# A hash-masked attention kernel with a feed-forward layer: first pair prepared head by head, two more pairs hashed together, and every part of the preparation placed anew

## The chip, the cores and the metric

The kernel runs on one core of a Trainium2 chip. The metric is the device time of one execution in microseconds (us), the median of several. The profile of a kernel is one such execution; its span is about 1.8 us shorter than the device time of the same execution. The engines are TensorE (PE; PEld are its weight loads), VectorE (DVE), ScalarE (ACT), GpSimd (POOL) and SyncE (SP), which here only issues DMAs.

A program on one core shows no second die to compare with, so the state of an execution is judged by its time and by its granted TensorE clock.

## The reference

Attention with a hash as its mask, then a feed-forward layer with the activation h + sin²(αh)/α:

```python
q_bits = (np.einsum('bhsd,dk->bhsk', q, proj) > 0)       # 6 bits; k the same
mask = q_bucket[:, :, :, None] == k_bucket[:, :, None, :]
scores = scale * np.matmul(q, k.transpose(0, 1, 3, 2))
scores = np.where(mask, scores, -1000000000.0)
attn = softmax(scores)                                    # cut
x = np.matmul(attn, v)            # batch 4, heads 8, 768 positions, 64 wide
h = x @ w_in                      # 3072 x 512 by 512 x 2048
g = h + np.sin(alpha * h) ** 2 / (alpha + 1e-09)
return g @ w_out                  # 3072 x 512
```

## The kernel before

The 32 heads are worked in 16 pairs, four pairs to a batch. A pair takes 12 attention steps; a step is one score tile (768 queries by 128 keys), one Exp on ACT and, three steps later, one weighing by the values. After pairs 4, 8, 12 and 15 come 16 steps of the feed-forward layer's first product for the batch before, each with one Sin. Steps are counted through: pairs 0 to 4 are steps 0 to 59, the first feed-forward stretch is 60 to 75, pair 5 is 76 to 87, pair 6 is 88 to 99, pair 9 begins at 140, and so on up to 239; the last 16 Sins follow. The second product is cut into single matmuls, and one or two of them are put into each attention step as filling.

Each pair needs preparation: load, turn (DVE transposes), cast to 16 bits (POOL), hash (PE), find the bits (DVE), and bring queries and keys with their bits into an operand buffer in transposed form. Pairs 0 to 5 are flipped on PE. Pairs 6 to 15 use DMA transposes, a write of the bit rows to memory and a read back. All of these are placed by a table, `PLAN`, from part and pair to a step number; the parts of one step are put into the program after that step's Exp:

```python
for key, when in sorted(PLAN.items(), key=lambda kv: (kv[1], kv[0])):
    at.setdefault(int(when), []).append(key)
...
def go():
    for key in at.pop(now[0], ()):
        part(key)
    now[0] += 1
...
# kinds of part: lq lk lv load; tq tk turn; cq ck cast queries, keys; cv sv cast, sum values;
# hash, bits; rows write bit rows; rq rk read them back; Tq Tk DMA transposes;
# mq mk move the second head; f00..f11 flips on PE; base; wl wc load, cast weights
```

So a step number sets an order in each engine's list. It sets no time. Every buffer is one of a small ring, and a part that takes a buffer waits for the last reader of what lay in it:

```python
hash_pool = ctx.enter_context(tc.tile_pool(name="hash", bufs=2))
aug_pool = ctx.enter_context(tc.tile_pool(name="aug", bufs=3))    # operand buffers qa, ka
v_pool = ctx.enter_context(tc.tile_pool(name="vp", bufs=4))       # values, 16 bits
...
def transpose_by_dma(i, t):
    nc.sync.dma_start_transpose(out=aug_of(i)[t][:, 0, :]..., in_=nats[i, t]...)   # cut
def move_second_head(i, t):
    a = augs[i][t]
    nc.vector.tensor_copy(out=a[0:64, 1, :], in_=a[64:128, 0, :])
```

All DMAs of loads, transposes, rows and results are issued by SP, in one ordered list.

The softmax here doesn't subtract the row's maximum and nothing guards it: scores larger than these inputs give would overflow.

## Time and profile before

| | before |
|---|---|
| median of the first three executions | 315.48 us (313.41 to 316.59) |
| span of the profiled execution | 314.0 us |
| PE / ACT / DVE / POOL busy | 298.0 / 237.9 / 201.4 / 98.2 us |
| first Exp, step 12, first Sin (step 60) | 10.52, 22.49, 63.51 us |
| first feed-forward stretch (steps 60 to 78) | 24.39 us |
| mean granted clock of the profiled execution | one slice of 40 at 0.7, the others full |

PE is busy 95% of the span, so the time can only fall where PE waits or runs at half clock. Read the table by steps: the difference of two step times is the cost of that stretch. This is the view of groups by form of the kernel before, DVE only, from 61 to 93 us: line, engine, operation, output and input, count, then busy us and mean ns, then idle time before.

```profile
L560 DVE SCALAR_TENSOR_TENSOR g<-s,inv_alpha,banks 128x768 bf16<-128x768 bf16 x16 | 16.1, 1014 | 1.1 <-ACT s L588 0.2
L590 DVE TENSOR_TENSOR s<-s 128x768 bf16<-128x768 bf16 x9 | 5.7, 632 | 0.0
```

The stretch's own DVE work is 16 closings (g) and 9 squares, 21.8 us of some 24.4.

### The profile page before, as it was taken

The page shows a single profiled execution, that of the slowest core. Times are in us where ns is not written, and L with a number is a line of the kernel's source. Part 1 is how long each engine was busy: PE and PEld are TensorE (multiplying, and loading weights), DVE is VectorE, ACT ScalarE, POOL GpSimd, SP SyncE. Part 2 cuts the span into 40 slices and gives each one's busy share as a digit, 9 for nine tenths or more (in the row PEclk, how much of TensorE's full clock was granted, in tenths as well). Part 3 has the DMA queues.
Part 4 walks back from the last instruction along what each step waited for, and adds up shares of the span by engine and source line. Part 5 has one row for each costly group of instructions (what it writes and reads, how often), then busy time and mean ns, then how long its engine had stood idle before and what let it go on. Part 6 is the DMA issues. An engine that isn't in the chain of part 4 may idle for free.

```text
span 314.0 us, 7658 instructions
## 1 busy us (share of the span) xinstructions
PE 298.0 (95%) x3026; PEld 184.5 (59%) x3055; DVE 201.4 (64%) x348; ACT 237.9 (76%) x295; POOL 98.2 (31%) x180
## 2 busy tenths in 40 slices
PE   7799989899999998899999999999999999999996
PEld 6467767566555565565656666566556655555444
DVE  4587676689956922769983753869973324499411
ACT  1589989799887788469988878869988887499200
POOL 6757488426695432515000605320000000000000
PEclk9999999999999999799999999999999999999999
DMA  7935989999737596781007697881006202200021
GB/s 232 378 117 157 240 280 294 148 279 252 255 78 214 98 215 163 188 223 26 2 0 201 140 233 126 227 106 21 0 35 106 69 20 76 58 2 0 31 102 70
DMA packets 68724, 42.87 MB, mean 137 GB/s; under 512 B 46560, under 2 KB 63696, under 8 KB 68688
## 3 DMA queue, kind: packets, MB, share of 16 engines
q1 hardware_dynamic: 68576, 42.37, 52.4%
q8 instruction: 24, 0.39, 0.5%
q14 instruction: 12, 0.10, 0.1%
q10 hardware_dynamic: 112, 0.01, 0.0%
HBM read 28.01 MB, written 7.27 MB: 112 GB/s over the span
## 4 chain that ended last, share of the span: by engine, by line
PE 80%; DVE 10%; DMA 3%; issue 2%; POOL 2%; ACT 1%; SPq 0%; DVEq 0%; POOLq 0%; ACTq 0%
PE banks L573 25%; PE banks L608 23%; PE banks L538 16%; PE banks L518 10%; PE banks L293 4%; PE banks L398 2%; DVE qt L284 1%; DMA ka<-kn 1%; DVE g L560 1%; DVE osb L616 1%; DMA proj_sb<-in_proj_dram 1%; DVE kt L284 1%; DMA xt<-xn 1%; DVE qa L400 1%; DVE xn L492 1%
## 5 line engine op out<-in xcount | busy, mean ns | idle before, releaser
L545 ACT ACTIVATE e<-banks 128x768 bf16<-128x768 f32 x192 | 147.7, 813 | 34.7 <-PE banks L538 28.7
L608 PE MATMUL banks<-w_out_bf,g 128*128 128x512 bf16 (+1 forms) x371 | 99.3, 372 | 4.7 <-DVE osb L616 3.3
L538 PE MATMUL banks<-qa,ka 76*128 76x384 bf16 x384 | 93.2, 326 | 0.6 <-DVE ka L400 0.5
L573 PE MATMUL banks<-xt,w_in_bf 128*128 128x384 bf16 x512 | 85.2, 326 | 0.5 <-DVE g L560 0.3
L518 PEld LDWEIGHTS <-e 128*128 128x128 bf16 x1152 | 55.7, 98 | 27.9 <-issue 1.4
L573 PEld LDWEIGHTS <-w_in_bf 128*128 128x128 bf16 x512 | 49.7, 98 | 33.8 <-issue 1.0
L560 DVE SCALAR_TENSOR_TENSOR g<-s,inv_alpha,banks 128x768 bf16<-128x768 bf16 x64 | 64.2, 1013 | 5.2 <-ACT s L588 1.8
L582 ACT ACTIVATE s<-banks,alpha_sb 128x768 bf16<-128x768 f32 x64 | 57.2, 893 | 11.4 <-PE banks L573 9.2
L518 PE MATMUL banks<-vaug,e 128*128 128x65 bf16 x1152 | 62.0, 194 | 0.3
L608 PEld LDWEIGHTS <-g 128*128 128x128 bf16 x400 | 38.6, 97 | 35.8 <-issue 5.3
L486 DVE TENSOR_TENSOR total<-banks,base 128x390 f32<-128x390 f32 x28 | 15.7, 561 | 45.1 <-PE banks L518 44.9
L325 POOL CAST vaug<-v 128x768 bf16<-128x768 f32 x16 | 13.6, 850 | 72.5 <-PE banks L518 32.3
L538 PEld LDWEIGHTS <-ka 76*128 76x128 bf16 x384 | 28.3, 98 | 8.5 <-issue 0.3
L616 DVE COPY osb<-banks 128x512 f32<-128x512 f32 (+1 forms) x25 | 16.7, 668 | 24.5 <-PE banks L608 23.4
L588 ACT ACTIVATE s<-s 128x768 bf16<-128x768 bf16 x29 | 24.5, 843 | 0.9
L590 DVE TENSOR_TENSOR s<-s 128x768 bf16<-128x768 bf16 x35 | 20.9, 597 | 1.9 <-ACT s L582 1.9
L335 POOL TENSOR_TENSOR vacc<-vacc,vaug 128x130 f32<-128x130 f32 x48 | 20.8, 433 | 3.8
L284 DVE STREAM_TRANSPOSE qt<-q 128x768 f32<-128x768 f32 x16 | 15.3, 959 | 2.3 <-DMA q<-in_q_dram 2.3
L492 DVE TENSOR_TENSOR xn<-total,rden 128x384 bf16<-128x384 f32 x28 | 16.1, 575 | 1.0
L293 PE MATMUL banks<-qt,w_hash 128*32 128x192 f32 x128 | 12.9, 331 | 2.5 <-DVE base L342 0.8
L284 DVE STREAM_TRANSPOSE kt<-k 128x768 f32<-128x768 f32 x16 | 15.1, 945 | 0.1
L293 PE MATMUL banks<-kt,w_hash 128*32 128x192 f32 x128 | 12.7, 330 | 0.4 <-DVE kt L284 0.4
(63 smaller groups left out, 177.6 us busy)
## 6 DMA issues: line engine op xcount, KB each, us to landing
q<-in_q_dram SPq DMA_DIRECT2D x16, 384.0 KB
k<-in_k_dram SPq DMA_DIRECT2D x16, 384.0 KB
v<-in_v_dram SPq DMA_DIRECT2D x16, 384.0 KB
out_dram<-osb SPq DMA_DIRECT2D x23, 256.0 KB
w<-in_moe_w_in_dram SPq DMA_DIRECT2D x8, 512.0 KB
w<-in_moe_w_out_dram SPq DMA_DIRECT2D x8, 512.0 KB
rows<-bits SPq DMA_DIRECT2D x40, 24.0 KB
qa<-rows SPq DMA_DIRECT2D x20, 18.0 KB
```

The costliest lines, as they stand in the source:

```text
L284: nc.vector.transpose(out=t.rearrange("p h s b c -> p (h s b c)"), in_=src.rearrange("p h s d -> p (h s d)"),)
L293: nc.tensor.matmul(out=ps[32 * j:32 * j + 32, 0:SB * 32].rearrange("p (s c) -> p s c", s=SB), lhsT=w_hash[:, blk].rearrange("p l a -> p (l ...
L335: nc.gpsimd.tensor_tensor(out=dst, in0=vacc[:, sb % 2], in1=vaug[:, :, sb], op=ALU.add)
L518: nc.tensor.matmul(out=regions[:, qb * (D + 1):(qb + 1) * (D + 1)], lhsT=e[:, qb * 128:(qb + 1) * 128], rhs=vaug[:, hh, kb, :], start=(apa ...
L538: nc.tensor.matmul(out=sc[:, half, 0:HALF], lhsT=ka[0:KA, hh, kb * 128:(kb + 1) * 128], rhs=qa[0:KA, hh, half * HALF:(half + 1) * HALF], s ...
L545: nc.scalar.activation(out=e.rearrange("p (h c) -> p h c", h=2), in_=sc[:, :, 0:HALF], func=AF.Exp, scale=SCALE,)
L560: nc.vector.scalar_tensor_tensor(out=g[:, F, :].rearrange("p (h c) -> p h c", h=2), in0=s2.rearrange("p (h c) -> p h c", h=2), scalar=inv_ ...
L573: nc.tensor.matmul(out=h[:, half, 0:HALF], lhsT=w_in_bf[:, p, F * 128:(F + 1) * 128], rhs=xt[b][:, p, half * HALF:(half + 1) * HALF], star ...
L582: nc.scalar.activation(out=s.rearrange("p (h c) -> p h c", h=2), in_=h[:, :, 0:HALF], func=AF.Sin, scale=alpha_sb[:, F:F + 1],)
L588: nc.scalar.activation(out=s2, in_=s, func=AF.Square)
L590: nc.vector.tensor_tensor(out=s2, in0=s, in1=s, op=ALU.mult)
L608: nc.tensor.matmul(out=o, lhsT=g[:, F, sub * 128:(sub + 1) * 128], rhs=w_out_bf[:, F, c0:c1], start=(F == 0), stop=(F == NF - 1),)
```

## The change

The intent, as it can be read from the diff: let the first pair start sooner by preparing one head before the other, with its queries and keys loaded first; hash pairs 2, 3 and 6, 7 together; and give each part the place that a schedule model found for it. The table keeps its form, but nearly every number in it is new. The diff is cut to its core; the tables of pairs 6, 8, 10 and 12 stand for all.

```diff
 for name, when in dict(          # pair 6
-    lq=30.0241, lk=30.0242, lv=30.0243, cv=51.0066, sv=51.0067, tq=54.0068, tk=54.0069,
-    cq=54.007, ck=54.0071, Tq=54.0072, Tk=54.0073, hash=58.0074, bits=58.0075, rows=58.0076,
-    base=58.0077, mq=77.0078, mk=77.0079, rq=79.008, rk=79.0081,
+    lk=0.04, lv=0.13, lq=0.16, cq=16.01, ck=22.02, cv=31.01, tk=36.01, tq=41.01, sv=42.01,
+    Tq=51.04, Tk=54.01, base=55.02, hash=57.01, bits=60.01, mq=61.01, mk=64.03, rows=69.01,
+    rk=71.02, rq=72.02,
 # pair 8
-    cq=94.0103, ck=94.0104, Tq=94.0105, Tk=94.0106, hash=98.0107, bits=98.0108, ...
+    cq=75.02, Tk=75.05, Tq=77.01, hash=79.01, bits=80.01, cv=80.02, mq=88.01, ...
 # pair 10
-    cv=115.0133, ..., cq=118.0137, ck=118.0138, Tq=118.0139, Tk=118.014, ...
+    ck=80.04, cv=90.01, Tk=99.02, cq=102.01, Tq=108.01, ...
 # pair 12
-    cv=155.0167, ...
+    cv=100.01, ...
-HASHED = {8: (8, 9), 10: (10, 11), 12: (12, 13), 14: (14, 15)}
+HASHED = {8: (8, 9), 10: (10, 11), 12: (12, 13), 14: (14, 15), 2: (2, 3), 6: (6, 7)}
+SQUARES = ('DDADDADAADADADAD', 'AADDADADADAADADD')
+RATES = (1.8397, 1.9304)
+DUMMIES = (23, 6, 6, 0)
...
-        load(0, "q")
-        hash_constants()
-        load_alpha()
-        load(0, "kv")
+        nc.scalar.dma_start(out=proj_sb, in_=proj)
+        load(0, "qk", slice(0, 1))
+        load(0, "qk", slice(1, 2))
+        hash_constants()
...
+        under_way = prepare_first()      # a generator: head 0 now, head 1 in parts later
+        next(under_way)
```

## The prediction

> **What bounds the kernel now.** I read the page's busy table and slices first, to find the busiest engine; then busy times by stretch, to see where it is not full; then TensorE's waits and the timeline at the two places where the stretches show a hole.
>
> ```profile
> PE 298.0 (95%) x3026; PEld 184.5 (59%) x3055; DVE 201.4 (64%) x348; ACT 237.9 (76%) x295; POOL 98.2 (31%) x180
> ...
> PE   7799989899999998899999999999999999999996
> ...
> PEclk9999999999999999799999999999999999999999
> ```
>
> TensorE is busy 95% of 314.0 us, and there is one slice (the seventeenth, 125.6 to 133.4 us) with a granted clock of 0.7. A busy PE need not be a full one, so I add up what its stream must take from the spacing of matmul starts in the trace: scores 384 x 0.162 = 62.2; weighing by values 1152 x 0.029 = 33.4; first feed-forward product 512 x 0.162 = 82.9; second 368 x 0.216 + 32 x 0.109 = 83.0; hashes 8 pairs alone x 0.86 and 4 twos x 1.44 = 12.6; head transposes 144 x 0.056 = 8.1; bit picks 6 x 0.33 = 2.0; base rows 14 x 0.067 + 4 x 0.17 = 1.6. Sum 285.8 us. Real work starts at 5.9 us and the last matmul ends at 310.9, so 305 us are used: about 19 us are lost in the stream, 6 before it and 3 (last copy and store) after it. The change hardly touches the sum, so its gain must come out of these 28.
>
> ```profile
> 0.00:10.50 10.50, 7.52 (x113) 6.50 (x114) 5.15 (x17) 2.28 (x3) 7.69 (x28) 1.00 0.83 271
> 10.50:22.50 12.00, 10.32 (x167) 6.75 (x166) 9.34 (x17) 9.06 (x13) 6.73 (x12) 1.00 0.65 225
> ...
> 51.00:61.60 10.60, 8.81 (x154) 6.16 (x143) 7.95 (x17) 8.44 (x13) 7.25 (x12) 1.00 0.92 186
> 61.60:84.30 22.70, 22.35 (x150) 13.44 (x150) 20.01 (x26) 20.52 (x25) 9.96 (x9) 1.00 1.00 289
> ...
> 112.30:138.00 25.70, 23.08 (x248) 13.96 (x251) 13.30 (x27) 17.74 (x23) 9.47 (x18) 0.93 0.77 183
> 138.00:159.60 21.60, 21.55 (x146) 13.06 (x146) 19.53 (x26) 19.59 (x23) 5.27 (x9) 1.00 0.19 41
> ```
>
> Columns: the stretch, its length, then busy time of PE, weight loads, DVE, ACT and POOL, clock, DMA share, GB/s. The holes in PE are at the start, before 61.6 and in 112 to 138. The two stretches of the feed-forward layer (61.6 to 84.3, 138.0 to 159.6) have nearly none, but there DVE and ACT are both at 88 to 91%.
>
> ```profile
> PE banks L608 <- DVE osb L616: 3.3, 3, 2.3
> ...
> PE banks L340 <- DVE bits L371: 0.9, 1, 0.9
> PE banks L293 <- DVE base L342: 0.8, 1, 0.8
> PE banks L398 <- DVE nat L385: 0.7, 1, 0.7
> PE banks L293 <- DVE qa L400: 0.7, 1, 0.7
> PE banks L293 <- DVE xn L492: 0.6, 1, 0.6
> ```
>
> Columns: who waits for whom, total us, times, longest. All are waits for DVE: PE takes its instructions in order and stands before one part of the preparation (hash, pick, flip) whose DVE predecessor is not through. The longest, 2.3 us:
>
> ```profile
> 121.12 1.29 SPq L412 DMA_TRANSPOSE ka<-kn  x1
> ...
> 125.56 0.35 DVE L427 COPY ka<-ka 64x768 bf16<-64x768 bf16 x1 [2.57 <-DMA ka<-kn]
> 125.83 0.68 DVE L616 COPY osb<-banks 128x512 f32<-128x512 f32 x1
> ...
> 126.56 1.23 PE L608 MATMUL banks<-w_out_bf,g 128*128 128x512 bf16 x3 [2.34 <-DVE osb L616]
> ```
>
> DVE is held by a copy of pair 9's keys that needs a DMA transpose issued only at 121.12; behind it stands the eviction that frees PE's output bank. The chain of waits goes further back: POOL's value cast for pair 9 began at 114.87, then its sums and casts, then the transpose.
>
> **What the Trainium skill says.** "TensorE: Matmul & The Clock Gate", the section "Part 1: The HAM clock gate", has a matmul stream at half clock until some 3.4 us of activity, spaced by N/2.4 + 2.5 ns after. The trace agrees: the warm-up matmuls are 107 ns apart until 3.94 us and 56 ns after; 384 columns 162 ns, 512 columns 216 ns. The page wants an idle window of about 3.4 us for the fall back; here 2.5 us of idle before 126.56 were enough, as 512-column matmuls are 427 ns apart afterwards, until about 130.3. The same page's "Architectural detail" section calls ACT and DVE strict FIFO; the blocked eviction above is that. "ScalarE: Activation LUTs", section "What ACT_TABLE_LOAD costs", gives an ACTIVATE 186 + 0.833 N ns (826 for 768), 93 more with a pointer operand, and back-to-back ones overlap by about 93: the trace has 813 (Exp), 893 (Sin, a pointer scale) and 147.7/192 = 0.769 us per Exp in a row. "DMA: Bandwidth & Descriptors", section "Latency and other measured facts", puts a fixed cost of about 2 us on a DMA: the first 384 KB of queries, issued at 0.74, were usable at 4.04.
>
> **The change part by part.**
>
> *Start.* Before: queries at 4.04, two DVE transposes of 0.97 until 6.07, hash weights by eight POOL copies 4.32 to 6.12, hash done 7.0, bits 7.44, pick and its copy 8.38, flips and copies, first score 9.99, first Exp 10.52. After: one head of q and k is the same 384 KB, so both by about 4.1 (estimate from the old landing); half transposes of 0.49 until 4.7; hash weights by two tiny matmuls and one DVE product (proj is there at 4.2), about 4.95; hash of two rows about 0.65, 5.6; bits 0.42, 6.1; pick 0.33 and a half-sized copy 0.3, 6.9; two flips of 0.34 and a 0.55 copy, 8.3. First score near 8.4, Exp near 8.9: 1.6 us. The warm-up shrinks from 44 dummies to 23 + 6 + 6, which may leave part of this at half clock, up to 0.5 us: I take 1.3.
>
> *Pairs 0 to 4 (60 attention steps).* An Exp cadence of 0.769 makes 46.1 us of ACT; from 10.52 to the end of the sixtieth Exp at 62.2 it took 51.7, so 5.6 are lost: 2.7 in the first 12 steps (22.49 - 10.52 - 9.23), 2.8 in the other 48 (39.7 - 36.9). In the first 12 steps DVE is the limit. I counted its parts after the change: three half or split pieces of pair 0's second head 0.49 + 0.3 + 0.42 + 0.3, its two copies 1.1, pair 1's transposes 1.9, bits and pick copy 0.9, four copies 2.2, and four transposes of pairs 2 and 3, 3.8: 11.4 us against 9.2 of Exp. Thus the head start is mostly eaten there: step 12 some 1.2 us earlier, not 3. The later waits (0.8, 0.9, 0.7, 0.6 us) are what a placement can mend; I give 2.0 of the 2.8. Hashing 2, 3 and 6, 7 together saves 2 x (2 x 0.86 - 1.44) = 0.6 on PE, inside that. Pairs 0 to 4 in sum: 3.2.
>
> *First and second feed-forward stretch.* Square counts are unchanged (7 on ACT and 9 on DVE; 8 and 8 in the last). But DVE gets a key transpose of 0.95, two moves of 0.35 to 0.4 and two copies of 0.55 in the first stretch, and up to five moves, 1.8, in the second, where it already ran without a gap from 140.5 to 162.3. Part falls in its idle while the first Sin is awaited (1.7 and 1.3 us). I charge 0.3 + 0.5 = 0.8.
>
> *The stall of pair 9.* Its query cast goes from plan position 106 to 50, keys to 80, transposes to 86 and 88, the key move to 135. This removes 2.34 us of idle and the half clock of 126.56 to 130.3, that is 3.7/2 = 1.9: 4.2. The parts that come in its place have longer leads, so I give it nearly whole: 4.0.
>
> *The rest.* Waits of 0.5 and 0.6 us at 82 to 89 and 0.5 at 257.8; the faster fill (1.84 instead of 1.75 matmuls a step) only shifts PE work that must be done anyway. I take 1.0. Base rows folded in at the last key block instead of the first: no cost, only a later need.
>
> Sum: 3.2 (the start is in it, by way of step 12) + 4.0 + 1.0 - 0.8 = 7.4. 315.5 - 7.4 = 308.1, rounded 308.0. I add nothing for new waits and nothing for those that I leave standing and a plan searched against a model may have closed: they pull opposite ways.
>
> **Rivals.** (1) New waits eat the gain. For it: many parts lie close to their need (row reads of pair 12 at position 175 for a start at 176, of pair 15 at 227 for 228; weight casts at 75 to 77 just as the second product begins), and the DMA queue is one ordered line in which early loads stand before buffers that come free late. Against it: each engine runs through its own list, so a late position need not be a late time, and PE is up to three score tiles ahead of ACT. Result 311 to 316. (2) DVE becomes the bound in the feed-forward stretches: 20.9 us of its own work for 16 chunks against PE's 20.8, plus the added 2 to 3. Result 310 to 312. (3) The plan fills nearly all holes: ACT's floor met in pairs 0 to 4 (another 2 us), all single waits gone. Result 303 to 305. I hold the middle likelier than any of the three, and (3) likelier than (1), since most of the gain sits in two visible places.
>
> **Range and chances.** 2% is 6.3 us, a time of 309.2. My centre lies 1.2 under it with an uncertainty of about 3.5 (the three runs of before spread over 3.2 us alone). That gives faster 0.64, within 0.34, slower 0.02; eight in ten: 303.5 to 312.
>
> **What would show it.** First Exp near 8.9 us; step 12 near 21.3; first Sin near 60.3 instead of 63.5; no DVE wait of over 1 us for a DMA transpose and no slice of clock 0.7; feed-forward stretches 0.3 to 0.5 longer, DVE above 92% in them. Wrong if PE shows new waits for row reads, weight casts or evictions of over 2 us in sum, or a second fall of the clock.

## The result, and the profile after

The kernel after took 330.35 us (median of 4: 326.68 to 334.58) against 315.21 for the kernel before beside it (median of 4). The ratio is 1.0445, with a 95% interval of 1.0334 to 1.0556: slower. Ratios in this document are the mean time of one kernel's fast runs over that of the other's fast runs of the same rounds, so they are not quite the ratio of the medians that are quoted.

The header, the busy row of PE and the row of the granted clock on the page of the kernel after, in 40 slices of 8.2 us:

```profile
span 327.8 us, 7715 instructions
...
PE 303.6 (93%) x3047; PEld 185.9 (57%) x3074; DVE 205.5 (63%) x361; ACT 238.4 (73%) x297; POOL 96.2 (29%) x173
...
PEclk9999999999999799997999999999999999999999
```

PE's busy time grew by 5.6 us although its work is nearly the same, which fits the falls of the clock: there are now two slices at 0.7 where the kernel before had one. TensorE's waits in the kernel after (who waits for whom, total us, times, longest):

```profile
PE banks L701 <- DVE g L688: 3.6, 3, 1.7
PE banks L646 <- DVE total L615: 3.0, 1, 3.0
PE banks L701 <- DMA xt<-xn: 2.7, 2, 2.4
PE banks L367 <- POOL vsum L362: 2.7, 3, 1.0
PE banks L666 <- DMA ka<-rows: 1.4, 1, 1.4
...
PE banks L666 <- DMA qa<-rows: 0.8, 1, 0.8
```

All six are over their counterparts of before, and they sum to 14.2 us. The same loss, by the start times of single steps (Exp or Sin) in the two profiles:

| step | before | after | after minus before | added since the line above |
|---|---|---|---|---|
| 0 | 10.52 | 10.34 | −0.18 | |
| 12 | 22.49 | 22.79 | +0.30 | +0.48 |
| 60, first Sin | 63.51 | 64.06 | +0.55 | +0.25 |
| 78, end of the first feed-forward stretch | 87.90 | 93.08 | +5.18 | +4.63 |
| 90 | 99.81 | 105.13 | +5.32 | +0.14 |
| 96 | 105.47 | 115.32 | +9.85 | +4.53 |
| 120 | 132.62 | 141.60 | +8.98 | −0.87 |
| 156 | 175.60 | 189.10 | +13.50 | +4.52 |
| 255, last Sin | 290.94 | 304.72 | +13.78 | +0.28 |

Three places hold most of the loss: the first feed-forward stretch, the middle of pair 6, and the stretch from 142 to 153 us. Two rows need care. The profile of before has its own stall between steps 96 and 120: they took 27.15 us there and 26.28 after, but 24.03 in before_cv6 below, which is spared that stall. So the −0.87 hides a loss of some 2 us. And of the last 4.52, only 1.90 lie in steps 120 to 126, where the third place is, and 0.21 in steps 126 to 138. The other 2.41 lie in steps 138 to 156. There the kernel after hashes pairs 12 and 13 at place 150, which before did at 162; the prediction's sum has 1.44 us for such a hash. That work is only done earlier, but steps 156 to 188 did not get shorter by it (33.28 us against 33.15).

*The first feed-forward stretch.* Groups by form of the kernel after, DVE only, 61 to 93 us:

```profile
L688 DVE SCALAR_TENSOR_TENSOR g<-s,inv_alpha,banks 128x768 bf16<-128x768 bf16 x16 | 15.8, 1012 | 0.9
L718 DVE TENSOR_TENSOR s<-s 128x768 bf16<-128x768 bf16 x9 | 7.0, 782 | 0.6 <-ACT s L710 0.5
L311 DVE STREAM_TRANSPOSE kt<-k 128x768 f32<-128x768 f32 x2 | 1.9, 970 | 0.0
L398 DVE TENSOR_SCALAR bits<-banks,side 128x192 bf16<-128x192 f32 x4 | 1.4, 388 | 0.0
L469 DVE COPY qa<-qa 64x768 bf16<-64x768 bf16 x2 | 1.4, 683 | 0.1
```

These are the costliest groups. Over all groups of the two views, the last column (idle time) falls from 3.5 to 1.6 us. Busy time from 2.5 us before the first Sin to step 78, first before, then after (the stretch, its length, then PE, weight loads, DVE, ACT, POOL, clock, DMA share, GB/s):

```profile
61.01:87.90 26.89, 26.54 (x178) 15.63 (x178) 23.64 (x32) 24.31 (x28) 13.22 (x13) 1.00 0.87 249
61.56:93.08 31.52, 27.53 (x188) 16.07 (x187) 29.82 (x40) 24.90 (x30) 17.18 (x20) 1.00 0.91 251
```

PE was busy 99% of it before; after, DVE is the busiest, with 95%, and PE's waits on g follow. (If single instructions are added up, whose ends overlap, DVE has 24.9 and 31.6 us.)

*The middle of pair 6.* Three timelines of the kernel after, SP's queue, DVE and PE: start, us, instruction, count, and in brackets the idle time and what ended it.

```profile
91.05 0.91 SPq L204 DMA_DIRECT2D v<-in_v_dram  x2
102.45 2.25 SPq L454 DMA_TRANSPOSE ka<-kn  x1
104.75 1.28 SPq L454 DMA_TRANSPOSE qa<-qn  x1
```

```profile
107.64 0.94 DVE L469 COPY qa<-qa 64x768 bf16<-64x768 bf16 x1 [5.19 <-DMA qa<-qn]
108.51 0.97 DVE L469 COPY ka<-ka 64x768 bf16<-64x768 bf16 x1
109.50 0.57 DVE L615 TENSOR_TENSOR total<-banks,base 128x390 f32<-128x390 f32 x1
```

```profile
110.12 0.53 PE L646 MATMUL banks<-vaug,e 128*128 128x65 bf16 x12 [2.95 <-DVE total L615]
```

For over 10 us SP issues nothing. The head of its list is the key transpose of pair 8, at place 75.05. Counted in the order of allocation, it takes the operand buffer of pair 5, which is read until step 87. The score matmuls of that step end at 102.42 us in the trace, and the transpose goes out at 102.45. The query transpose follows at 104.75. DVE's list has the moves of pair 8 at place 88, so DVE stands 5.19 us for that DMA, and behind the moves stands `total`, which PE needs at 110.12. PE's matmuls then stood at twice their spacing until about 114.5 us.

*From 142 to 153 us.* POOL, SP and PE of the kernel after:

```profile
121.36 1.05 POOL L352 CAST vaug<-v 128x768 bf16<-128x768 f32 x1 [12.10 <-PE banks L646]
...
134.83 0.83 POOL L352 CAST vaug<-v 128x768 bf16<-128x768 f32 x1
...
138.41 0.82 POOL L347 CAST qn<-q 128x768 bf16<-128x768 f32 x1
```

```profile
139.26 1.22 SPq L454 DMA_TRANSPOSE qa<-qn  x1
...
141.66 1.22 SPq L626 DMA_TRANSPOSE xt<-xn  x1
```

```profile
147.26 0.97 PE L701 MATMUL banks<-xt,w_in_bf 128*128 128x384 bf16 x5 [2.45 <-DMA xt<-xn]
```

The value cast at 134.83 is pair 12's, at place 100.01. It takes the value buffer of pair 7, whose last weighing ends at 134.77 us. The query cast of pair 10 stands behind it on POOL, the transpose of pair 10 behind that cast on SP, and behind that the transpose of the attention result, xt, which the second feed-forward stretch needs. It landed at 147.2, with PE idle 2.4 us and at half clock until about 152.

### The profile page after: what moved, and what is told of

It is laid out like the page before. It is cut to its first block, busy times and chain, and to the rows that moved or that the text cites.

```text
span 327.8 us, 7715 instructions
## 1 busy us (share of the span) xinstructions
PE 303.6 (93%) x3047; PEld 185.9 (57%) x3074; DVE 205.5 (63%) x361; ACT 238.4 (73%) x297; POOL 96.2 (29%) x173
## 4 chain that ended last, share of the span: by engine, by line
PE 58%; DVE 14%; POOL 9%; DMA 7%; issue 6%; ACT 4%; SPq 1%; DVEq 0%; ACTq 0%; POOLq 0%
PE banks L736 20%; PE banks L701 14%; PE banks L666 12%; PE banks L646 7%; DVE g L688 5%; POOL vacc L362 3%; DVE s L718 3%; PE banks L320 3%; DMA xt<-xn 3%; ACT s L710 2%; DMA qa<-qn 2%; DVE qt L311 1%; DMA v<-in_v_dram 1%; ACT s L716 1%; PE banks L530 1%
## 5 line engine op out<-in xcount | busy, mean ns | idle before, releaser
L701 PE MATMUL banks<-xt,w_in_bf 128*128 128x384 bf16 x512 | 87.8, 330 | 6.6 <-DVE g L688 3.6
L688 DVE SCALAR_TENSOR_TENSOR g<-s,inv_alpha,banks 128x768 bf16<-128x768 bf16 x64 | 63.0, 1012 | 8.1 <-ACT s L716 4.7
L666 PEld LDWEIGHTS <-ka 76*128 76x128 bf16 x384 | 27.6, 98 | 12.3 <-issue 4.4
L718 DVE TENSOR_TENSOR s<-s 128x768 bf16<-128x768 bf16 x35 | 22.1, 630 | 0.8 <-ACT s L710 0.5
L621 DVE TENSOR_TENSOR xn<-total,rden 128x384 bf16<-128x384 f32 x28 | 16.3, 581 | 1.7 <-DMA xt<-xn 0.8
L320 PE MATMUL banks<-qt,w_hash 128*32 128x192 f32 x128 | 14.1, 336 | 1.5 <-DVE qt L311 0.6
L311 DVE STREAM_TRANSPOSE kt<-k 128x768 f32<-128x768 f32 x15 | 14.4, 960 | 1.4 <-PE banks L320 1.4
L311 DVE STREAM_TRANSPOSE qt<-q 128x768 f32<-128x768 f32 x15 | 14.4, 962 | 0.3
L347 POOL CAST qn<-q 128x768 bf16<-128x768 f32 x10 | 10.2, 1016 | 13.6 <-DMA qa<-qn 13.6
```

The costliest lines, as they stand in the source:

```text
L311: nc.vector.transpose(out=t.rearrange("p h s b c -> p (h s b c)"), in_=src.rearrange("p h s d -> p (h s d)"),)
L320: nc.tensor.matmul(out=ps[32 * j:32 * j + 32, 0:SB * 32].rearrange("p (s c) -> p s c", s=SB), lhsT=w_hash[:, blk].rearrange("p l a -> p (l ...
L666: nc.tensor.matmul(out=sc[:, half, 0:HALF], lhsT=ka[0:KA, hh, kb * 128:(kb + 1) * 128], rhs=qa[0:KA, hh, half * HALF:(half + 1) * HALF], s ...
L688: nc.vector.scalar_tensor_tensor(out=g[:, F, :].rearrange("p (h c) -> p h c", h=2), in0=s2.rearrange("p (h c) -> p h c", h=2), scalar=inv_ ...
L701: nc.tensor.matmul(out=h[:, half, 0:HALF], lhsT=w_in_bf[:, p, F * 128:(F + 1) * 128], rhs=xt[b][:, p, half * HALF:(half + 1) * HALF], star ...
L718: nc.vector.tensor_tensor(out=s2, in0=s, in1=s, op=ALU.mult)
```

## The experiments

Fifteen kernels ran, all correct. The theory after the result was: the loss is a set of separate places, each of which asks for a buffer, a queue or DVE too early. Rivals: the new start or the new filling is at fault; POOL slows DVE; or the new order has no slack at all, so that a removed wait only uncovers the next.

A warning on the ratios: the kernel before that ran beside an experiment had medians from 313.2 to 315.8 us, so small differences between ratios of different rounds mean nothing. The kernel after was not run again in these rounds.

### Is it the start, the early pairs, or the filling?

**start_only**: the new start and the new table for pairs 0 and 1, all else (places, filling, squares, hashes apart) as before.

```diff
 # kernel after, pairs 2 to 15 and the weights: the table of before put back, for example
-    ck=1.01, cv=3.03, cq=4.01, first=4.07, tk=5.03, tq=8.01, ...      # pair 2
+    tq=5.001, cq=5.0011, ck=5.0012, tk=7.0013, hash=11.0014, ...
```

> The new start (pairs 0 and 1, head by head, new hash weights, fewer warm-up matmuls) with the old places of all other parts, the old fill and squares, pairs 2,3 and 6,7 hashed apart. Theory A (the placement of the later parts costs the 15 us, the start is nearly neutral, since its first Exp is at 10.34 us against 10.52): 314 to 316 us, ratio to before 0.995 to 1.005, and the old stall of 2.3 us before an output product at about 126 us is back. Rival B (the split start costs more than its own stretch shows, through later buffers): slower than before by over 1%, 319 or more.

316.85 us (313.63 to 319.81), ratio 1.0004 (0.9901 to 1.0107): the start gains nothing and loses nothing that shows, in the two fast executions of four. The old stall is back in its profile with 1.52 us, not 2.3. The profiled execution was a slow one: the score matmuls stood 0.32 us apart until 20.5 us and 0.17 apart afterwards, so PE ran at half clock for its first 10 us of attention.

**early_new**: the new table for pairs 0 to 5 and the weights, that of before for pairs 6 to 15. The edit is as above, with other lines of the table.

> New start and new places for pairs 0 to 5 and for the weight loads and casts; old places for pairs 6 to 15, old fill and squares. Theory A (losses come from narrow places of the later pairs): first Sin at about 64 us as in the changed kernel, the first feed-forward stretch some 1 us longer than before, then like before, and the stall at 126 us is gone because pair 5's values are cast ahead of pair 6's here: 313 to 316 us. Rival B (the early part and its weight casts carry most of the loss): 322 or more.

317.67 us (314.65 to 321.86), ratio 1.0031 (0.993 to 1.0133). Steps 60 to 78 took 27.18 us in its profile, against 24.39 before and 29.02 after. That is 2.8 us more than before, where 1 was expected. So more than half of the first stretch's loss comes with the early pairs and the weights; the flips of pair 5 fall into it. The total time stays level with before, so most of the loss needs the later pairs.

**old_fill**: the kernel after with the filling and the squares of before.

```diff
-SQUARES = ('DDADDADAADADADAD', 'AADDADADADAADADD')
-RATES = (1.8397, 1.9304)
+SQUARES = ('DADADADADADADADD', 'DADADADADADADADA')
+RATES = (1.75, 1.9)
```

> The changed kernel with the old fill rates (1.75, 1.9) and the old order of squares. Theory A (placement): no change, 328 to 332 us. Rival C (the new order of squares starves the first feed-forward stretch, or the faster fill collides): the stretch loses its 3.6 us of TensorE waits on g, and the time falls to 326 or less.

332.06 us (327.93 to 335.91), ratio 1.0486. The filling is not the cause.

**warm44**: start_only with the longer warm-up of before, to see whether the half clock at the start comes from the shortened one.

```diff
-DUMMIES = (23, 6, 6, 0)
+DUMMIES = (44, 6, 6, 0)
```

> The kernel with the new start and the old places (start_only), with 44 instead of 23 matmuls to warm TensorE up. Theory (with 23 the clock is still half when the first hash comes, and in some executions stays half until about 17 us, which costs 3 to 5 us: start_only took 313.6, 315.1, 318.6 and 319.8): hash matmuls of pair 0 at half the time, first Exp at 9.3 to 10.0 us, and all executions within 2 us, median 312.5 to 314.5. Rival (the spread has another cause): executions above 318 stay.

316.93 us (314.52 to 318.75, 6 executions), ratio 1.0124 (1.0075 to 1.0173). In its profile the hash matmuls of the first head ran 0.16 us apart in place of 0.32 and the first Exp came at 10.05 us, but the executions of 318 us stayed. The profiled one (318.19 us) is one of them, and it lost its time later: its scores stood 0.16 us apart from the start, step 12 came at 22.44, and steps 12 to 78 took 68.68 us (65.41 before). So the half clock of the start is not the only cause of slow executions. Whether 44 matmuls prevent it in every execution is not shown.

### The operand buffer and the value buffer

**aug4**: a fourth operand buffer, with two other rings made smaller for room.

```diff
-    aug_pool = ctx.enter_context(tc.tile_pool(name="aug", bufs=3))
+    aug_pool = ctx.enter_context(tc.tile_pool(name="aug", bufs=4))
-    e_pool = ctx.enter_context(tc.tile_pool(name="ep", bufs=6))
+    e_pool = ctx.enter_context(tc.tile_pool(name="ep", bufs=5))
-    o_pool = ctx.enter_context(tc.tile_pool(name="op", bufs=4))
+    o_pool = ctx.enter_context(tc.tile_pool(name="op", bufs=2))
```

> The changed kernel with four buffers instead of three for the query and key operands of a pair; to make room, two instead of four output buffers and five instead of six for the weights e, which can only slow it. Places untouched. Theory A1 (the DMA queue stands before transposes of pairs 8 to 11 whose operand buffer is still read by the pair three before it): the queue's wait of 12 us before the key transpose of pair 8 goes, the move of pair 8 no longer holds DVE for 5.2 us, the 3.0 us wait of TensorE at 110 us and the half clock after it go, and step 96 is reached some 4 us earlier than in the changed kernel: 322 to 326 us. Rival (that wait is only taken over by the next thing in the queue): less than 1.5 us gained.

326.26 us (323.03 to 328.31), ratio 1.0449; the span of the profile fell from 327.8 to 321.2 us. SP's queue in aug4:

```profile
93.02 1.24 SPq L454 DMA_TRANSPOSE ka<-kn  x1
94.31 1.36 SPq L454 DMA_TRANSPOSE qa<-qn  x1
```

Pair 8's transposes go out 9.4 and 10.4 us earlier, the wait of 3.0 us and the fall of the clock behind it are gone, and steps 84 to 96 take 10.87 us instead of 15.64. (Other profiles with three operand buffers and much the same parts in these steps have 12.9 to 15.6 us, so the gain differs by execution.)

**ctrl4**: only the two smaller rings, the operand ring left at 3.

```diff
-    e_pool = ctx.enter_context(tc.tile_pool(name="ep", bufs=6))
+    e_pool = ctx.enter_context(tc.tile_pool(name="ep", bufs=5))
-    o_pool = ctx.enter_context(tc.tile_pool(name="op", bufs=4))
+    o_pool = ctx.enter_context(tc.tile_pool(name="op", bufs=2))
```

> The kernel after with only the two rings made smaller that aug4 had made smaller to get room (operand ring op from 4 to 2, exponentials e from 6 to 5), and the 3 operand buffers left at 3. Theory (aug4's 5 to 6 us in the profile came from the fourth buffer): no gain here, span 327 to 332 us, ratio 1.045 to 1.055, and the 3.0 us wait of TensorE on the totals near 110 us with the half clock after it is still there. Rival (the smaller rings, by another placing in memory or another order of releases, made the gain): span near 321 us and the wait near 110 us gone.

330.94 us (329.25 to 331.71), ratio 1.058, span 327.5, with a wait of 2.7 us on `total` at pair 6. The fourth operand buffer made aug4's gain: 4.7 us between the two medians.

**cv_late**: the kernel after, with the value casts of pairs 12, 13 and 14 (and what hangs on them) moved behind the release of the buffers that they take.

```diff
+MOVED = {
+    ('cv', 12): 115.01, ('sv', 12): 115.02, ('base', 12): 123.03, ('cv', 14): 127.01,
+    ('sv', 14): 127.02, ('cv', 13): 155.01, ('sv', 13): 155.02, ('lv', 15): 116.01,
+    ('cq', 12): 121.01, ('cq', 14): 122.03,
+}
+PLAN.update(MOVED)
```

> The changed kernel with the value casts and sums of pairs 12, 14, 13 (and the query casts of 12 and 14, the base row of 12, the load of v of 15) at places where the buffer that they take is free. Theory A2 (POOL, in order, stands before casts whose buffer is held for 14 to 50 further steps, which delays pair 10's query cast, with it the DMA queue's next transpose and the transpose of pair 7's result that the second feed-forward stretch needs): the wait for that transpose at 147 us (2.45 us) and the half clock after it, and the wait for a value sum at 132 us (1.0) go: 4 to 5 us, 324 to 327 us. Rival: DMA transposes are slow by themselves there (5.5 us from issue to use): the wait stays.

328.97 us (325.32 to 330.68), ratio 1.0475, span 323.5. The wait of 2.4 us on xt is gone. In its place PE waited on g there, 1.28 and 0.31 us. The xt transpose was issued at 135.13 us in place of 141.66, so the link from the value buffer to it is shown; that the time came back whole is not. Steps 120 to 138 took 25.71 us against 27.36, a gain of 1.65, where 4 to 5 were expected. Of the 4.3 us that the span fell, 2.6 lie in pair 6, which this edit does not touch.

### The first feed-forward stretch

**f0_dve**: DVE work of pairs 5 and 6 moved out of the stretch.

```diff
+MOVED = {
+    ('mq', 6): 77.06, ('mk', 6): 77.07, ('rk', 6): 79.01, ('rq', 6): 79.02, ('f00', 5): 53.01,
+    ('f01', 5): 54.02,
+}
+PLAN.update(MOVED)
```

> The changed kernel with four DVE parts taken out of the first feed-forward stretch: the moves of pair 6 behind it, the flips of pair 5's first head before it. Theory A3 (DVE is the bound of that stretch through the number of its instructions): 1.1 us for the two copies and 1.7 for the two moves, steps 60 to 78 some 2.5 us shorter than in the changed kernel (29.0 us there, 24.4 before): 327 us. Rival A4 (it is the sharing with POOL): under 1.7 us.

The stretch fell from 29.02 to 25.88 us, as the theory of a DVE bound wants. The time rose all the same to 337.16 us (336.61 to 337.64), ratio 1.0775. TensorE's longest wait in it, and SP's queue:

```profile
PE banks L672 <- DMA qa<-rows: 8.9, 2, 8.4
```

```profile
103.34 1.24 SPq L460 DMA_TRANSPOSE ka<-kn  x1
```

(The profile also has a start at half clock, with step 12 at 26.20 us.) I had moved pair 6's row reads behind the blocked transpose of pair 8. A miss of mine, but a clear one: one line of the queue that waits for a buffer holds up everything behind it, here for 8.4 us.

**f0_pool**: POOL work meant to move out of the stretch, DVE's left.

```diff
+MOVED = { ('cv', 7): 77.2, ('sv', 7): 77.3, ('lv', 10): 78.02 }
+PLAN.update(MOVED)
```

> The changed kernel with the value cast and sums of pair 7 moved from the first feed-forward stretch to behind it (POOL parts only, 3.5 us of POOL). Theory A4 (DVE instructions with two operands in SBUF, and fast copies, wait for POOL: squares took 937 ns beside POOL and 554 alone): two squares and one move get shorter, 1 to 1.5 us off the stretch: 328 to 329 us. Theory A3: no change.

328.44 us (326.86 to 330.71), ratio 1.0503. The stretch took 28.72 us, 0.3 less than after, and the squares fell from 782 to 725 ns on average. But the test failed: POOL ran ahead and did the moved value cast at 83.72 us, still inside the stretch, and was busy there for 19.2 us where the kernel after has 17.2. And 0.3 us is within the spread of profiles that left this stretch alone (28.14 in aug4, 28.17 in cv_late, 28.69 in ctrl4). What POOL costs DVE is not measured by this run.

### Sum of the repairs, or no slack?

**repaired**: aug4, cv_late and f0_dve together, with four single places more.

```diff
+# MOVED of cv_late and of f0_dve, and:
+    ('rk', 12): 174.015, ('base', 4): 54.03, ('base', 5): 55.03, ('base', 6): 60.06,
```

> All repairs on the changed kernel at once: four operand buffers, late value casts (12, 13, 14), the four DVE parts out of the first feed-forward stretch, base rows of pairs 4, 5 and 6 after their value sums are done, and the last row read of pair 12 ahead of a DMA transpose and the row writes of pair 13 in the queue. Theory (the loss is the sum of these separate waits): 2.0 us less before step 60, 3 in the first stretch, 5 at step 90, 3 to 4 between steps 108 and 132, 1.5 at step 176; 327.8 - 15 = about 313 us in the profile, 313 to 317 timed, ratio to before 1.00 to 1.01. Rival (one wait only hides the next, the plan has no slack anywhere): above 320 us.

327.58 us (323.55 to 327.95), ratio 1.0477. All three old waits were gone, and three others had come: 1.65 us on pair 6's row reads at 101 us with half clock after it, 0.98 on a value sum, 1.82 at 204 us. Taken alone this speaks for the rival, whose span of over 320 us also came (321.8). But the first of them lay at the place that f0_dve had already shown to be wrong.

**repaired2**: the row reads of pair 6 back at their places, the moves of pair 6 before the stretch, three `base` products later, one set of bits later.

```diff
-    ('mq', 6): 77.06, ('mk', 6): 77.07, ('rk', 6): 79.01, ('rq', 6): 79.02,
+    ('mq', 6): 58.05, ('mk', 6): 58.06,
+    ('base', 9): 118.01, ('base', 8): 119.01, ('base', 10): 121.02, ('bits', 14): 178.5,
```

> The repaired kernel again, with my own two mistakes in it taken out: the row reads of pair 6 stay at their places 71 and 72 of the kernel after, and only the merged moves of pair 6 into the operand buffers go to position 58; the number bits of pair 14, which wait for a ring of two row buffers, come 3 places later; the products of pairs 4 to 6 and 8 to 10 stand 1 to 3 places later so that each takes a buffer already released. Theory (the waits are separable, each is one place that asks for a buffer or a queue too early): of the 7.8 us that the span of repaired (321.8 us) was over the kernel before, the 1.65 us wait and the half clock after it near step 90 (together 4.8 us), and about 1.6 us at step 203 go; span 313 to 316 us, ratio to before 1.00 to 1.015, and no TensorE wait over 1 us on the row reads. Rival (the new order has no slack, one wait only hides the next): span above 319 us, ratio above 1.025, with at least one new wait over 1 us that the list of repaired does not have.

323.3 us (322.68 to 324.24), ratio 1.0331, span 321.2: by its numbers the rival's case. DVE's timeline at the new wait:

```profile
66.53 0.57 DVE L479 COPY ka<-ka 64x768 bf16<-64x768 bf16 x1 [3.42 <-DMA ka<-kn]
```

The key transpose of pair 6 landed only at 66.5 us. The move that I had placed at 58 held DVE for it, PE waited 4.2 us for the `base` copy behind it, and half clock followed until about 75. Step 66 came 7.3 us later than in the kernel before, and the span ended 7.2 us later. No other wait was over 1.1 us.

**repaired3** and **repaired4**: repaired2 with only that place changed, in two ways.

```diff
-    ('mq', 6): 58.05, ('mk', 6): 58.06,
+    ('mq', 6): 76.003, ('mk', 6): 76.004, ('rk', 6): 76.005, ('rq', 6): 76.006,     # repaired3
```

```diff
-    ('mq', 6): 58.05, ('mk', 6): 58.06,                                # repaired4: as in after
```

> repaired2 with one thing changed: the two moves of pair 6 and its row reads stand together at position 76, at the end of the first feed-forward stretch and ahead of the 8 row writes that stood before them in the queue in repaired. In repaired2 the moves stood at 58, the vector engine waited 3.42 us for the transposed keys and TensorE 4.2 us behind it, with half clock after it, together 7.0 us (step 66: 7.3 us later than in the kernel before). Theory (separable): all of these 7 us go and no new wait over 1 us comes; steps 60 to 78 take 25.5 to 26.5 us, and the span is 313.5 to 316 us, ratio 1.00 to 1.015. Rival (no slack): span above 318 us, with a new wait over 1 us elsewhere.

> repaired2 with the two moves of pair 6 at the places of the kernel after (61 and 64, inside the first feed-forward stretch). Theory (separable): the 7.0 us of repaired2 at step 66 go, and the vector engine's extra work in the stretch shows again, so steps 60 to 78 take 27 to 28 us; span 316 to 318 us, ratio 1.01 to 1.02, some 1 to 2 us above repaired3. Rival (no slack): span as in repaired2, 320 us or more.

repaired3: 317.84 us (316.7 to 318.64), ratio 1.0125 (1.002 to 1.0229), span 314.9. repaired4: 320.5 us (318.57 to 323.47), ratio 1.0181 (1.0049 to 1.0312), span 316.8. The first stretch took 24.29 us in repaired3 (24.39 before; expected 25.5 to 26.5) and 27.19 in repaired4. TensorE's longest waits in repaired3:

```profile
PE banks L540 <- DVE empty L245: 1.1, 1, 1.1
PE banks L676 <- ACT e L683: 1.1, 3, 0.5
PE banks L656 <- DVE total L625: 1.0, 1, 1.0
```

The first is the warm-up at the very start, which the kernel before has too. No new wait over 1 us came, and the clock was full in all four executions. So most of the loss was a sum of separate places: 12.5 us of median (1.0445 and 1.0125 in ratio) lie between the kernel after and repaired3, which has the same parts, the same start and, but for 24 numbers of the table and three ring sizes, the same plan. But the rest of the gain that was hoped for is not there. repaired3 comes level with the profiled execution of before (314.9 and 314.0 us), and that one had a stall and a fall of the clock which about half of the executions of before are spared.

The step times place the rest. Against the profile of before_cv6 (310.8 us, no stall of over 0.8 us there) repaired3 is 0.2 us ahead at step 78, 0.4 behind at 126, 1.9 at 138, 4.1 at 156 and 4.0 at 255. Steps 126 to 138, in the second feed-forward stretch, took 17.13 us against 15.69. DVE was busy for 16.3 of these 17.1 us and PE for 16.1; four moves of second heads (1.7 us) stand among them, which before_cv6 does not have there. This is the prediction's rival (2) in the second stretch. The 2.2 us between 138 and 156 are mostly the hash of pairs 12 and 13, done earlier there as in the kernel after; steps 156 to 188 got only 0.2 us shorter for it (32.94 against 33.16), and PE, full there in before_cv6, was idle for 1.0 us. No run tests these two readings.

### The stall of pair 9 in the kernel before

**before_cv6**: the kernel before, with the value cast of pair 6 put behind pair 5's. The theory was that pair 9's stall comes from a value buffer handed out in the wrong order, so that POOL is late.

```diff
-    lq=30.0241, lk=30.0242, lv=30.0243, cv=51.0066, sv=51.0067, tq=54.0068, tk=54.0069,
+    lq=30.0241, lk=30.0242, lv=30.0243, cv=52.00621, sv=52.00622, tq=54.0068, tk=54.0069,
```

> The kernel before, with one part moved: the value cast and sum of pair 6 behind those of pair 5 (position 52 instead of 51), so that the ring of four value buffers is taken in the order of pairs. Theory: the value cast of pair 9 then waits for pair 5's buffer, free long before, instead of pair 6's, starts some 9 us earlier, and the chain cast, sums, casts, transpose, move, eviction no longer stops TensorE at 126 us: no slice of clock 0.7 there and 310.5 to 312 us, ratio 0.985 to 0.990. Rival: the stall moves to the next late pair and the gain is under 1 us.

313.1 us (312.61 to 314.25), ratio 0.997 (0.9903 to 1.0036), span 310.8, and PE's wait at the stall only 0.8 us, with no fall of the clock in the profile. That looks like a hit. The timelines of POOL and DVE in before_cv6 say otherwise:

```profile
114.65 0.83 POOL L325 CAST vaug<-v 128x768 bf16<-128x768 f32 x1 [9.07 <-PE banks L538]
```

```profile
123.85 0.35 DVE L427 COPY ka<-ka 64x768 bf16<-64x768 bf16 x1 [0.95 <-DMA ka<-kn]
```

POOL waits 9.07 us to 114.65, as it waited 9.08 to 114.87 before, so the edit changed nothing there. The key transpose was issued at 121.02 (121.12 before) and used 2.83 us later, where the kernel before needed 4.44. The landing of one DMA differed, and with it the stall. The theory fell. Counting the casts shows a mistake of reading too: of 16 value casts the one at 114.87 is the eleventh, so it is pair 10's. Pair 9's queries and keys had been cast by 105.8; its transposes stood in SP's list behind pair 8's row reads (117.96), which had waited 2.3 us for the written rows.

If the stall is a matter of one landing, it should come and go. Beside these experiments the kernel before ran 58 times. Its mean granted clock was 1.000 in 29 executions (median 312.8 us), 0.995 in 20 (median 314.7), 0.999 or 0.993 in 4, and below 0.99 in 5 (318 to 320). One short fall of the clock, as in the profile, makes about 0.995. So such a fall was in the profile that the prediction was made from, and absent in half of all executions.

**tuned**: before_cv6 with the moves and row reads of pair 9 placed behind the copy that frees PE's output bank, and one `base` later. It keeps the start and the places of before otherwise.

```diff
-    ... rows=108, base=109.5, mq=113.0129, mk=113.013, rq=115.0131, rk=115.0132,     # pair 9
+    ... rows=108, base=109.5, mq=117.0129, mk=117.013, rq=119.0131, rk=119.0132,
-    base=58.0077, ...                                                                # pair 6
+    base=60.0077, ...
```

> The kernel before with the ring of value buffers in order (before_cv6) and two more parts later: the moves and row reads of pair 9 four places later, behind their DMA transposes, and the base row of pair 6 two places later. Theory: the stalls of 0.8 us at 125 us and 0.9 at 60.5 us go, 309 to 310 us in the profile, 310 to 312.5 timed, ratio 0.985 to 0.993: a little better than both kernels. Rival: the moves come too near to pair 9 and TensorE waits there instead, no change from before_cv6 (312.6 to 314.3).

312.19 us (311.12 to 313.46, 22 executions) against 313.86 (312.06 to 319.27, 29 executions) for the kernel before; ratio of fast runs 0.9967 (0.9951 to 0.9983), span 309.3. DVE's timeline in tuned:

```profile
122.70 0.69 DVE L616 COPY osb<-banks 128x512 f32<-128x512 f32 x1 [3.72 <-PE banks L608]
...
124.72 0.36 DVE L427 COPY qa<-qa 64x768 bf16<-64x768 bf16 x1
124.99 0.35 DVE L427 COPY ka<-ka 64x768 bf16<-64x768 bf16 x1
```

DVE now does the eviction first and finds both transposes landed afterwards. The gain in the mean of fast runs is 0.3%, within the 2% that counts as the same, but it is resolved, and none of the 22 executions was slow, where 5 of the 29 beside them were. The expected ratio of 0.985 to 0.993 was missed all the same. It is the fastest version of this study.

## Why the prediction was wrong

The prediction said 308.0 us and gave 0.02 to slower; 330.35 was measured. Point by point, the steps of its sum:

| step of the prediction | predicted | in the profiles |
|---|---|---|
| start, first Exp near 8.9 us | −1.6, of which 1.3 were taken | −0.18 (10.34) |
| step 12 near 21.3 | −1.2 | +0.30 (22.79) |
| pairs 0 to 4, first Sin near 60.3 | −3.2 | +0.55 (64.06) |
| first feed-forward stretch | +0.3 | +4.63 |
| second feed-forward stretch | +0.5 | +0.21 (15.65 to 15.86 for steps 126 to 138), but two of its moves ran right behind the stall, before step 126; 17.13 in repaired3, without that stall |
| stall of pair 9 | −4.0 | gone, but see below |
| the rest | −1.0 | +2.41 in steps 138 to 156, +0.28 after |
| new waits | 0 | six groups, 14.2 us, and two falls of the clock |

**The step that failed is "I add nothing for new waits".** It was named as rival (1) with the right symptoms: row reads close to their need, one ordered DMA queue, "early loads stand before buffers that come free late". Its weight against it was "a late position need not be a late time". The runs showed the converse, which the prediction did not draw: an early position need not be an early time, and it can do harm. A part that asks for a buffer before its release stops its whole engine or queue, and with it parts that another engine needs. The prediction read the diff for how close each part stood to its need; it did not check for each part whether the buffer that it takes was free at that place. Counted afterwards from the table and the ring sizes (an estimate, which takes each ring in the order of its allocations), dozens of allocations of the kernel after stand before the release of what they take; in the kernel before only two or three do, by at most three steps. Not each of them costs time. aug4 and ctrl4 show that it does for the operand buffers of pair 8 (4.8 us in the profiles), and cv_late for the value buffer of pair 12. repaired3 shows that all of it together with the first stretch is worth 12.5 us, of which the first stretch has 4.7. Rival (1) was right in kind, and its 311 to 316 us was far too narrow.

**The first feed-forward stretch** was mis-sized, with the mechanism right (rival 2). The charge of 0.3 us counted a transpose, two moves and two copies and let "part fall in its idle". Measured from 2.5 us before the first Sin to step 78, the kernel after has three transposes of 0.92 to 0.97 us more (2.9), two flip copies (1.1), two sets of bits (0.8), part of alpha's inversion (0.25), moves of 2.1 in place of 1.4, squares of 7.0 in place of 5.7, and less 0.3 for a base copy. That is 6.7 us more work in a stretch that had 2.0 us left over by the same way of adding up. repaired3 moved the flips of pair 5 and the moves of pair 6 out and was back at 24.29 us. It had help: its squares took 5.2 us in sum, 1.8 less than after, although POOL was as busy (17.4 us).

The squares show one thing that the prediction had not used, and no run isolates it. In the Trainium skill, "SBUF — State Buffer", the section "SBUF: two separate sides" has VectorE and GpSimd share one port pair as an exclusive lock, which a VectorE operation with two inputs from SBUF needs when GpSimd reads, and whoever comes second blocks. The trace agrees: over the whole execution a square without a POOL instruction beside it took 551 to 554 ns on average in both kernels, with one beside it 731 before and 937 after (longest 1278), while g, which has an input from PSUM, took 1014 and 1012. In the first stretch the longer squares are 1.35 of the 6.7 us.

**The start** was right in what it removes and wrong in its clock. The hash matmuls of the first head ran 0.32 us apart, as at half clock, and the bits were done at 6.92 us (predicted 6.1), the picked bits at 7.89 (6.9), the last copy before the first score at 9.77 (8.3). The charge of "up to 0.5 us" for half clock stands against delays of 0.8 by the bits and 1.5 by that copy. Not all of this is the clock: in warm44, with the hash at full rate behind a longer warm-up, the first Exp came only 0.29 us sooner. start_only finds no gain in the time (ratio 1.0004).

**Pairs 0 to 4**: steps 12 to 60 took 41.02 us before and 41.27 after. The 2.0 us of waits that "a placement can mend" were mended in part and replaced by waits for POOL's value sums (0.10, 0.68, 1.02 and 0.12 us between 36 and 59 us).

**Pair 9's stall**: it is gone, as predicted, and the condition that showed it, no slice of clock 0.7, failed all the same, since two new falls came. The sign "no DVE wait of over 1 us for a DMA transpose" failed too, with the 5.19 us in pair 6. The chain given for the stall, back to POOL's value cast, was a misreading (that cast is pair 10's), and the 2.5 us of idle that the prediction compares with the skill's window are 2.34 in the line that it shows. The size was a second error. The 4.0 us are real in the profiled execution, but executions of before without the fall of the clock have a median of 312.8 us. The time that a perfect cure saves is nearer 1 to 2 us; tuned, which is such a cure, moved the median of the fast runs by 1.2 (313.4 to 312.2).

The range of 303.5 to 312 followed from these steps, and none of its width came from the number of parts moved at once. The test that the prediction set itself did work: "new waits for row reads, weight casts or evictions of over 2 us in sum, or a second fall of the clock". The row reads alone came to 2.2 us.

What stays open: why the half clock of the start lasts in some executions and not in others, and whether the moves in the second stretch and the early hash of pairs 12 and 13 are the whole of the 4 us that repaired3, with all its waits at 1.1 us or less, still lacks (span 314.9, against 310.9 for the execution of before of 312.68 us beside it).

## What to carry to other kernels

When a plan moves parts earlier, check for each one what it takes, not only what it feeds: the ring's size and the last reader of that buffer tell from the table alone whether its engine or queue will stop there. On an engine or queue that works in order, put the instruction that waits for a DMA behind the one that frees a buffer for the busiest engine. And when one wait after another appears, judge "no slack" only after a version without misplaced parts of your own has run: repaired and repaired2 spoke for it, and repaired3 against it.

## What the Trainium skill lacked or had wrong

- "TensorE: Matmul & The Clock Gate" gives, in its table of the two states, an idle window of about 3.4 us before the clock falls. In the profiles PE fell to half clock after idle gaps of 2.34 us (before), 2.95 and 2.45 us (after) and 1.65 us (repaired, at 101 us).
- "TensorE: Matmul & The Clock Gate" warns that single clock-gate events of a trace can be unreliable; it has no case like this one, in which the granted clock in the records and the rate of PE differ: in start_only's profile the row of the granted clock is full while score matmuls stand 0.32 us apart until 20.5 us, twice the 0.16 to 0.17 after.
- "DMA: Bandwidth & Descriptors" lists constraints and a bandwidth of the DMA transpose and gives no latency for one of this size (128 by 768 elements of 2 bytes). Here 2.8 to 5.6 us passed from issue to the first use, and the same transpose took 2.83 us in one profile and 4.44 in another.
- "SBUF — State Buffer" fits with its lock; the runs add the size for a square of 128 by 768: 554 ns alone, 604 (repaired3) to 937 (after) on average beside POOL.
